# Gated mix of dilated window attention and a spatial-gating MLP: later loads of o and wo, and a maximum in three steps

## The chip, the core and the metric

The kernel runs on one core of a Trainium2 chip. The metric is the device time of one execution in microseconds (us), as the median of several runs. The engines are named as in the profile: PE (TensorE, matrix products; PEld is its weight load), DVE (VectorE), ACT (ScalarE), POOL (GpSimd) and SP (SyncE, which here only issues DMAs). Each takes its instructions in the order of the program; an instruction that waits holds up all those behind it on the same engine. A "q" behind the name (SPq, ACTq) is the engine's sequencer, which issues DMAs and waits.

## The reference

With x of 2048 rows and 1024 columns, all inputs bf16:

```python
g = sigmoid((x * gate_w).sum(-1, keepdims=True))
# A: 32 heads of 32; each position sees 8 keys, at its own place and 2, 4, ... 14 before it
q, k, v = split(x @ wqkv)
attn = softmax(where(in_range, einsum(q, k[window]) * 32 ** -0.5, -1e9))
a = (attn @ v[window]) @ wo
# B: a gated MLP with a 2048x2048 mixing over positions
z1, z2 = split(gelu(x @ w_in))                 # 1792 columns each
b = (z1 * (w_sp @ layernorm(z2) + b_sp[:, None])) @ w_out
out = g * a + (1 - g) * b
```

## The kernel before

**Stages on PE.** The order is: q, k, v for eight groups of four heads (`qkv_tile`, line 739) with part of z2 (`z2_tile`, line 339); the rest of z2; z1 (line 836); the mixing w_sp @ z2 (`g_group`, from about 366 us); the product of the attention's result o with wo (`wo_group`, from about 541 us); the product with w_out (from about 589 us). The last three do a 2x2 block product in seven products instead of eight, with sums and differences of blocks (s1 to s4, t1 to t4, h1 to h4) formed by DVE. All their matmuls are on line 853, in `product`.

**The attention** is not on PE. DVE does it for the eight head groups with multiplications and pairwise sums (lines 362 to 408), spread over the PE stages up to the middle of the mixing. `soft_a` takes the maximum over the 8 keys of a position and subtracts it; `att_L` holds 2 halves x 8 keys x 32 values in each of 128 partitions, in f32, and `att_m` is a small tile of 2 x 4 x 32 values, which `soft_b` uses later for the sums. The results of the groups go to DRAM (`o_d`) by `store_o`, from where transposing DMAs bring them back for `wo_group`: `load_heads(u, r)` on line 492, two for each of eight row blocks u.

**The mixing** has 16 groups n (u = n // 2 is the block of 256 rows, fb = n % 2 the half of the columns). Each group makes seven products of 8 matmuls, in the order a11, s1, s2, a12 (in the bank named `seed`), s3, s4, a22. ACT copies intermediate results out of PSUM (lines 877, 863, 865, 896, 865, 907). DVE adds two pairs (`vec`, line 869) and multiplies with z1 (line 908). The results sit in four ring slots (`g_ring`, which `y_ring` overlays). `y_finish(u)` scales the two groups of block u (lines 701 to 709), and `y_done(u)` stores them to `y_d` (line 652, two DMAs). The copy on line 896 is the first write of a group into its ring slot, so it needs the y store of the group four before it to have landed. The rows of w_sp for the next block come in by two transposing DMAs, `load_rows` on line 597; DVE scales them (`scale_rows`, line 604) and forms s1 to s4 (lines 608 and 609) before the block's first group.

**The order of the work** is fixed when the program is built. A planner, `Beat`, keeps a model clock `now` that moves on by each product's columns (1.52 us for each product of the mixing) and a model time `vector` up to which DVE has work. `beat.at(t, fn)` puts a piece of work at the model time t: it is emitted after the first product at whose end the clock has reached t, in order of t. `behind_mult` is a list that is worked off from its front at two places of a group: an entry (t, price, fn) is emitted if the clock has reached t and the price fits into the group's remaining room (7 us at the end of a group with fb = 1, 1.5 us at the end of the others, the rest of that in the middle of the next group). So the times in `attended` decide the place of each piece in the queues of SP, DVE and PE, and nothing of it is decided at run time.

**`attended`** is emitted at the model time 456.68, which is the start of group 9 and 464.5 us in the trace (so model times here are 7.9 us before the trace's). It stores the last group's o, loads wo, from a copy in DRAM whose rows were put in order earlier (2 MB, `load_wo`, line 566), and plans the loads of the first two blocks of o, the sum for o's scale (`o_total`, `o_matmul`, `o_power`), the scaling of wo in four pieces (`wo_scale`, line 538), the sums for block 0 (`heads_sums(0)`, lines 528 to 532) and two of the four differences of wo (`wo_sum`, line 543).

Of the kernel before, what the change touches and what calls it, by code (L numbers as in the profile page):

```python
# [24 lines left out]
W = 8  # L25
# [36 lines left out]
def kernel(  # L62
# [13 lines left out]
    nc = tc.nc  # L76
# [11 lines left out]
    def reg(off, n):  # L88
        return arena[:, off:off + n]
# [64 lines left out]
    att_m = sm.tile([P, 2, 4, 32], F32, name="att_m")  # L154
# [155 lines left out]
    beat = Beat()  # L310
# [40 lines left out]
    L = att_L  # L351
    L4 = L[:].rearrange("p (a w n) -> p a w n", a=2, w=W, n=32)
# [3 lines left out]
    TT = nc.vector.tensor_tensor  # L356
# [23 lines left out]
        return [(4.4, mul), (2.3, fold(16)), (1.2, fold(8)), (0.7, fold(4)), (0.4, fold(2)), (0.4, last)]  # L380

    def soft_a():
        nc.vector.tensor_reduce(att_m[:, :, 0, :], L[:].rearrange("p (a w n) -> p a n w", a=2, w=W), AX.X, ALU.max)
        TT(L4, L4, att_m[:, :, 0:1, :].to_broadcast([P, 2, W, 32]), ALU.subtract)

    def soft_exp():
# [34 lines left out]
    def store_o(g):  # L421
        dst = o_d[:, g * C:(g + 1) * C].rearrange("(p j) c -> p j c", j=NJ)
        sync.dma_start(dst, obuf)

    def attention_steps(t):
# [29 lines left out]
        for took, fn in pv_steps(NG - 1, 0) + pv_steps(NG - 1, 1):  # L455
            yield t + 5.0, took, fn
        t = beat.vector
        beat.at(t + 1.0, attended)

    beside_fork, beside_copy, behind_mult = [], [], []  # L460
# [11 lines left out]

    def attended():
        store_o(NG - 1)
        load_wo()
        o_norm(NG - 1, reg(A_OFF + 8192, 2048).rearrange("p (j c) -> p j c", j=NJ))
        prep["attended"] = True
        t = max(beat.now, beat.vector)
        plan_heads(0, t + 5.0, 3.0)
        plan_heads(1, t + 11.0, 3.0)  # L480
        beat.at(t + 5.0, o_total)
        behind_mult.append((t + 14.0, 0.0, o_matmul))
        behind_mult.append((t + 15.0, 0.9, o_power))
        for m in range(4):
            behind_mult.append((t + 10.0, 0.75, lambda m=m: wo_scale(m)))
        behind_mult.append((t + 13.5, 2.45, lambda: heads_sums(0)))
        for m in range(2):
            behind_mult.append((t + 13.5, 1.25, lambda m=m: wo_sum(m)))

    def load_heads(u, r):  # L490
        a = 2 * u + r
        sync.dma_start_transpose(heads[u].raw[r], o_d[a * P:(a + 1) * P, :])  # L492

    def plan_heads(u, t, pace):
        for r in range(2):
            beat.at(t + pace * r, lambda r=r: load_heads(u, r))

    def o_norm(g, waste):
        nc.scalar.activation(waste, obuf, ACT.Abs, accum_out=ol[:, g:g + 1])
# [26 lines left out]
    def heads_sums(u):  # L526
        v = heads[u]
        nc.vector.tensor_scalar(v.half, v.flat, osc[:, u:u + 1], None, ALU.mult)
        TT(v.s1, v.a21, v.a22, ALU.add)
        TT(v.s3, v.a11, v.a21, ALU.subtract)  # L530
        TT(v.s2, v.s1, v.a11, ALU.subtract)
        TT(v.s4, v.a12, v.s2, ALU.subtract)
        beat.on_vector(2.45)
        prep["heads"] += 1

    def wo_scale(m):
        sl = slice(2048 * m, 2048 * (m + 1))
        nc.vector.tensor_scalar(wo_h[:, sl], wo_n[:, sl], wsc[:, 1:2], None, ALU.mult)
        beat.on_vector(0.75)

    def wo_sum(m):
        out_, a, b = ((h1, c12, c11), (h2, c22, h1), (h3, c22, c12), (h4, c21, h2))[m]
        TT(out_, a, b, ALU.subtract)
        beat.on_vector(1.25)
# [20 lines left out]
    def load_wo():  # L565
        sync.dma_start(wo_n.rearrange("p (k n) -> p k n", n=D), wop_d.rearrange("(k p) n -> p k n", p=P))
# [197 lines left out]
    for n in range(L1_EARLY):  # L764
        t = beat.now + 8.0 + 13.0 * n
# [19 lines left out]
    t = beat.now  # L785
# [17 lines left out]
    for i in range(16):  # L803
        for c in range(1 if i > 2 else 2, 4):
            z2_tile(i, c)
        n = L1_EARLY + (i - 3) // 2
# [7 lines left out]
    t = beat.now  # L814
# [128 lines left out]
    for n in range(2 * NU):  # L943
        u, fb = n // 2, n % 2
        t = beat.now
# [23 lines left out]
    t = beat.now  # L969
# [174 lines left out]
```

## Time and profile before

| | us |
|---|---|
| median of 3 runs | 679.54 |
| lowest and highest | 678.07, 680.69 |
| the profiled execution's own time | 679.48 |
| its span, first to last instruction | 677.7 |
| PE busy in the span | 670.1 (99%) |
| DVE busy | 537.5 (79%) |
| ACT busy | 381.1 (56%) |
| TensorE clock granted, mean | 1.000 |

The times of rows in the trace are counted from the span's start. The profiled execution's time is 1.8 us longer than its span, and 0.06 us below the median. In a row of the timeline the columns are start, duration, engine, line and operation, what it writes and reads, the number of instructions merged into the row; in brackets how long the engine was idle before it and what ended that. A SPq row is a DMA's issue, not its transfer. "Landing" is the time at which the DMA's semaphore tells that all its data has arrived.

### The profile page before, as it was taken

How to read it: one execution, taken by the hardware profiler on the slowest of the kernel's cores; microseconds unless marked ns; L12 is line 12 of the kernel's file. 1: busy time of each engine (PE TensorE's matmuls, PEld its weight loads, DVE VectorE, ACT ScalarE, POOL GpSimd, SP SyncE). 2: the span in 40 equal slices, each digit the busy share in tenths (PEclk: the TensorE clock that was granted, in tenths of full speed). 3: DMA queues.
4: the chain of work that ended last, by engine and by line, in shares of the span. 5: the costliest groups of instructions: out<-in, count | busy, mean ns of one | idle time of the engine just before them, and what ended most of it. 6: DMA issues, size and time to landing. Idle time of an engine off the chain costs nothing.

```text
span 677.7 us, 9532 instructions
## 1 busy us (share of the span) xinstructions
PE 670.1 (99%) x3587; PEld 392.5 (58%) x3587; DVE 537.5 (79%) x588; ACT 381.1 (56%) x714; POOL 15.5 (2%) x68
## 2 busy tenths in 40 slices
PE   8999999999999999999999999999899999999997
PEld 4568688888885555555555555555455544444443
DVE  1007799999999999999999999997369587954745
ACT  4334646455645985979953666667555574522121
POOL 0000000000000002010100000000000000000000
PEclk9999999999999999999999999999999999999999
DMA  8979869988879754267545555949966699485211
GB/s 233 179 151 281 222 163 289 236 221 219 199 195 241 231 191 175 83 204 251 169 158 176 138 133 148 270 109 248 250 161 164 166 235 251 78 172 144 59 62 63
DMA packets 230734, 123.92 MB, mean 183 GB/s; under 512 B 191008, under 2 KB 217248, under 8 KB 230688
## 3 DMA queue, kind: packets, MB, share of 16 engines
q1 hardware_dynamic: 229104, 121.21, 68.6%
q10 hardware_dynamic: 1584, 2.10, 0.9%
q8 instruction: 28, 0.46, 0.3%
q14 instruction: 18, 0.15, 0.1%
HBM read 63.97 MB, written 37.82 MB: 150 GB/s over the span
## 4 chain that ended last, share of the span: by engine, by line
PE 95%; DMA 2%; SPq 2%; ACT 0%; issue 0%; DVE 0%; ACTq 0%
PE ps L853 36%; PE ps L739 18%; PE ps L339 11%; PE ps L836 11%; PE sd L739 6%; PE seed L853 6%; PE sd L339 4%; PE sd L836 4%; SPq L492 1%; DMA o_d<-arena 1%; DMA arena<-in_B_w_in_dram 1%; DMA y_d<-arena 0%; ACT arena L670 0%; SPq L720 0%; DVE arena L1011 0%
## 5 line engine op out<-in xcount | busy, mean ns | idle before, releaser
L853 PE MATMUL ps<-arena 128*128 128x448 f16 (+1 forms) x1296 | 264.4, 363 | 1.9 <-ACT arena L865 1.9
L853 PEld LDWEIGHTS <-arena 128*128 128x128 f16 x1512 | 147.8, 98 | 156.8 <-issue 2.6
L739 PEld LDWEIGHTS <-arena 128*128 128x128 bf16 x1024 | 141.7, 138 | 24.9
L739 PE MATMUL ps<-arena 128*128 128x384 bf16 x768 | 130.0, 326 | 0.0
L362 DVE TENSOR_TENSOR arena<-arena 128x8192 bf16<-128x8192 bf16 x16 | 70.8, 4422 | 43.9 <-DMA arena<-k_d 43.6
L339 PE MATMUL ps<-arena 128*128 128x448 bf16 (+1 forms) x384 | 77.9, 357 | 0.8 <-DMA arena<-in_B_w_in_dram 0.8
L742 ACT CAST arena<-ps 128x384 bf16<-128x384 f32 x96 | 45.1, 481 | 58.7 <-PE ps L739 58.7
L339 PEld LDWEIGHTS <-arena 128*128 128x128 bf16 x512 | 50.3, 99 | 47.3 <-issue 2.0
L836 PEld LDWEIGHTS <-arena 128*128 128x128 bf16 x512 | 50.0, 98 | 46.6
L366 DVE TENSOR_TENSOR arena<-arena 128x4096 bf16<-128x4096 bf16 (+1 forms) x64 | 74.1, 1158 | 2.0
L836 PE MATMUL ps<-arena 128*128 128x448 bf16 x384 | 75.4, 352 | 0.0
L402 DVE TENSOR_TENSOR arena<-arena,att_A 128x8192 bf16<-128x8192 bf16 x16 | 70.7, 4421 | 0.2
L853 PE MATMUL seed<-arena 128*128 128x448 f16 (+1 forms) x216 | 47.8, 363 | 0.0
L739 PE MATMUL sd<-arena 128*128 128x384 bf16 x256 | 46.8, 326 | 0.0
L408 DVE TENSOR_TENSOR arena<-arena 128x4096 bf16<-128x4096 bf16 x16 | 36.6, 2289 | 0.3
L345 ACT ACTIVATE arena<-ps 128x448 bf16<-128x448 f32 x48 | 26.2, 554 | 17.6 <-PE ps L339 17.3
L572 ACT ACTIVATE arena<-arena 128x2048 bf16<-128x2048 bf16 x16 | 30.8, 1922 | 8.1 <-DMA arena<-in_B_w_sp_dram 8.1
L1075 ACT ACTIVATE arena<-ps,omr 128x512 f32<-128x512 f32 x24 | 16.5, 688 | 32.7 <-PE ps L853 32.7
L839 ACT ACTIVATE arena<-ps 128x448 bf16<-128x448 f32 x48 | 25.1, 557 | 17.1 <-PE ps L836 16.0
L865 ACT ACTIVATE arena<-ps,bt 128x448 f32<-128x448 f32 x32 | 20.3, 634 | 21.9 <-PE ps L853 20.0
L1011 DVE SCALAR_TENSOR_TENSOR arena<-seed,omr,arena 128x512 bf16<-128x512 f32 x8 | 6.0, 750 | 32.7 <-PE seed L853 32.7
L696 ACT ACTIVATE arena<-arena 128x896 bf16<-128x896 bf16 x32 | 30.3, 946 | 1.0 <-DVE arena L908 0.5
(136 smaller groups left out, 602.3 us busy)
## 6 DMA issues: line engine op xcount, KB each, us to landing
arena<-in_B_w_sp_dram SPq DMA_DIRECT2D x16, 512.0 KB, 6.1
arena<-k_d SPq DMA_DIRECT2D x8, 960.0 KB, 7.1
arena<-v_d SPq DMA_DIRECT2D x8, 960.0 KB, 5.3
z_d<-arena SPq DMA_DIRECT2D x16, 448.0 KB, 3.1
arena<-z_d SPq DMA_DIRECT2D x16, 448.0 KB, 4.0
y_d<-arena SPq DMA_DIRECT2D x16, 448.0 KB, 3.6
arena<-in_A_wqkv_dram SPq DMA_DIRECT2D x24, 256.0 KB, 5.6
arena<-in_B_w_in_dram SPq DMA_DIRECT2D x6, 896.0 KB, 5.8
```

What stands on the lines that cost most here:

```text
L339: nc.tensor.matmul(ps[:, 0:N], xT[:, kt, i * P:(i + 1) * P], w2[:, kt, ZC * c:ZC * c + N], start=(kt == 0), stop=(kt == KT - 1))
L345: nc.scalar.activation(z2[:, i, ZC * c:ZC * (c + 1)], ps[:, 0:ZC], ACT.Gelu_apprx_tanh, accum_out=s1[:, 4 * i + c:4 * i + c + 1])
L362: TT(prod.rearrange("p (w j c) -> p w j c", w=W, j=8, c=C), in0, in1, ALU.mult)
L366: return lambda: TT(pv[:, :, 0:n], pv[:, :, 0:n], pv[:, :, n:2 * n], ALU.add)
L402: TT(prod.rearrange("p (w j d h) -> p w j d h", w=W, j=8, d=DH, h=HG), in0, in1, ALU.mult)
L408: return [(4.4, mul), (2.3, lambda: TT(p3[:, 0:4, :], p3[:, 0:4, :], p3[:, 4:8, :], ALU.add)), (1.2, lambda: TT(p3[:, 0:2, :], p3[:, 0:2, ...
L572: nc.scalar.activation(waste, slot, ACT.Abs, accum_out=l1[:, a:a + 1])
L696: nc.scalar.activation(waste, g_ring[n % 4][:, r], ACT.Abs, accum_out=yl[:, k:k + 1])
L739: nc.tensor.matmul(ps[:, 0:3 * C].rearrange("p (t c) -> p t c", t=3), lhsT, wgt[:, :, kt, :], start=(kt == 0), stop=(kt == KT - 1))
L742: nc.scalar.copy(st[:, j % 4, :].rearrange("p (t d h) -> p t d h", t=3, h=HG), ps[:, 0:3 * C].rearrange("p (t h d) -> p t d h", t=3, h=HG))
L836: nc.tensor.matmul(ps[:, 0:512 if whole and kt == 0 else ZC], xT[:, kt, i * P:(i + 1) * P], _sub_ap(w1, kt * ZC, [[1, 512 if whole and kt ...
L853: nc.tensor.matmul(ps[:, 0:c1 - c0], w[:, k, :], v[:, k, c0:c1], start=(first and k == 0), stop=(k == K - 1), skip_group_check=True)
```

## The change

`soft_a` takes the maximum over 8 keys by three element-wise maxima (8 to 4, 4 to 2, 2 to 1), in place of one reduction over a rearranged view. In `attended`, with t the model time there (456.68): the load of wo moves from at once to t + 10.5; the two loads of o's block 0 from t + 5 and t + 8 to t + 7 and t + 10; those of block 1 from t + 11 and t + 14 to t + 16 and t + 19; `o_total` from t + 5 to t + 6. In `behind_mult`, `heads_sums(0)` moves ahead of the four `wo_scale` and is due at t + 18 instead of t + 13.5; the four `wo_scale` are due at t + 24 instead of t + 10, the two `wo_sum` at t + 24 instead of t + 13.5.

```diff
     def soft_a():
-        nc.vector.tensor_reduce(att_m[:, :, 0, :], L[:].rearrange("p (a w n) -> p a n w", a=2, w=W), AX.X, ALU.max)
+        TT(att_m[:], L4[:, :, 0:4, :], L4[:, :, 4:8, :], ALU.max)
+        TT(att_m[:, :, 0:2, :], att_m[:, :, 0:2, :], att_m[:, :, 2:4, :], ALU.max)
+        TT(att_m[:, :, 0:1, :], att_m[:, :, 0:1, :], att_m[:, :, 1:2, :], ALU.max)
         TT(L4, L4, att_m[:, :, 0:1, :].to_broadcast([P, 2, W, 32]), ALU.subtract)
...
     def attended():
         store_o(NG - 1)
-        load_wo()
         o_norm(NG - 1, reg(A_OFF + 8192, 2048).rearrange("p (j c) -> p j c", j=NJ))
         prep["attended"] = True
         t = max(beat.now, beat.vector)
-        plan_heads(0, t + 5.0, 3.0)
-        plan_heads(1, t + 11.0, 3.0)
-        beat.at(t + 5.0, o_total)
+        plan_heads(0, t + 7.0, 3.0)
+        beat.at(t + 10.5, load_wo)
+        plan_heads(1, t + 16.0, 3.0)
+        beat.at(t + 6.0, o_total)
         behind_mult.append((t + 14.0, 0.0, o_matmul))
         behind_mult.append((t + 15.0, 0.9, o_power))
+        behind_mult.append((t + 18.0, 2.45, lambda: heads_sums(0)))
         for m in range(4):
-            behind_mult.append((t + 10.0, 0.75, lambda m=m: wo_scale(m)))
-        behind_mult.append((t + 13.5, 2.45, lambda: heads_sums(0)))
+            behind_mult.append((t + 24.0, 0.75, lambda m=m: wo_scale(m)))
         for m in range(2):
-            behind_mult.append((t + 13.5, 1.25, lambda m=m: wo_sum(m)))
+            behind_mult.append((t + 24.0, 1.25, lambda m=m: wo_sum(m)))
```

## The prediction

> **What bounds the kernel now.** I read the page's busy rows first, then PE's waits, then the chain and the timelines around the only wait that costs anything.
>
> ```profile
> PE 670.1 (99%) x3587; PEld 392.5 (58%) x3587; DVE 537.5 (79%) x588; ACT 381.1 (56%) x714; POOL 15.5 (2%) x68
> ```
>
> PE is busy for 670.1 of 677.7 us. The waits of PE over the whole span are three, and one lies in the part that changes:
>
> ```profile
> PE ps L853 <- ACT arena L865: 1.9, 1, 1.9
> PE pw L114 <- DVE arena L108: 1.2, 1, 1.2
> PE ps L339 <- DMA arena<-in_B_w_in_dram: 0.8, 1, 0.8
> ```
>
> So nothing here can win more than about 2 us. The timeline of PE, with the seed product (the fourth of seven) as a mark for each group, prices it:
>
> ```profile
> 469.08 1.68 PE L853 MATMUL seed<-arena 128*128 128x448 f16 x8
> 479.68 1.68 PE L853 MATMUL seed<-arena 128*128 128x448 f16 x8
> 486.32 6.21 PE L853 MATMUL ps<-arena 128*128 128x448 f16 x32 [1.94 <-ACT arena L865]
> 492.37 1.68 PE L853 MATMUL seed<-arena 128*128 128x448 f16 x8
> 503.02 1.68 PE L853 MATMUL seed<-arena 128*128 128x448 f16 x8
> ```
>
> A group takes 10.60 us (469.08 to 479.68), but 12.69 from group 10's seed to group 11's: 2.1 us lost. The chain of waits says why (SPq L492 are the loads of o):
>
> ```profile
> 465.88 5.16 DMA o_d<-arena
> 471.06 5.80 SPq L492
> 476.91 3.78 SPq L492
> 480.81 2.90 DMA y_d<-arena
> ```
>
> SP waits until the last o is in DRAM (471.04), then spends 5.80 and 3.78 us on issuing the two loads of o's block 0. Behind them stands the y store of block 3, whose data DVE had ready at 474.88 (line 709: 473.60 + 1.28). It lands at 483.7, and ACT's copy into the same ring slot has waited for it:
>
> ```profile
> 483.80 0.53 ACT L896 CAST arena<-seed 128x448 bf16<-128x448 f32 x1 [3.29 <-DMA y_d<-arena]
> 505.72 0.53 ACT L896 CAST arena<-seed 128x448 bf16<-128x448 f32 x1 [1.87 <-DMA y_d<-arena]
> ```
>
> The second row is group 12's: the same kind of wait two groups later, which costs PE nothing so far. What it hangs on is DVE's wait for the rows of w_sp of block 6:
>
> ```profile
> 494.56 1.23 DVE L604 TENSOR_TENSOR arena<-arena,rs_b 128x2048 f16<-128x2048 bf16 x1 [4.21 <-DMA arena<-in_B_w_sp_dram]
> 497.25 1.22 DVE L604 TENSOR_TENSOR arena<-arena,rs_b 128x2048 f16<-128x2048 bf16 x1 [1.46 <-DMA arena<-in_B_w_sp_dram]
> ```
>
> From 497.25 to 530 DVE has no gap, so all it does there, the y store of block 4 included (issued 502.99, landed 505.62), is pinned to the landing of these rows. SP's timeline shows what stood before them:
>
> ```profile
> 466.51 2.54 SPq L566 DMA_DIRECT2D arena<-wop_d  x1
> ...
> 481.89 2.25 SPq L492 DMA_TRANSPOSE arena<-o_d  x1
> 484.19 0.57 SPq L600 DMA_DIRECT2D rs_b<-rs_d  x1
> 484.85 0.38 SPq L646 DMA_DIRECT2D arena<-z_d  x1
> 485.33 8.64 SPq L597 DMA_TRANSPOSE arena<-in_B_w_sp_dram  x2
> ```
>
> **The change, part by part.**
>
> **The maximum.** The reduction (line 383, 400.06) is followed by the next instruction 1.08 us later. The three maxima have the shapes of lines 390 to 392, which take 0.42, 0.29 and 0.23 us and, with their gaps, 1.04 (421.50 to 422.54). If a maximum costs what an addition costs, DVE gains 0.04 us eight times, 0.3 in all. If it ran at the reduction's rate, 1.05 us for 512 elements, 448 elements in three would take 0.92 plus overheads, some 1.1: 0.2 lost in all. Either lies beside PE, which has no wait before 484; DVE ends the attention at 462.83 and soon idles 3.16 us before line 908 (467.06), which covers it. I take nothing.
>
> **Order on DVE and PE.** I followed the planner's arithmetic. `o_total` (t + 6 = 462.68) still comes out after the product that ends at 462.75. `o_matmul` and `o_power` are held by `w_total` and `w_power` ahead of them in the list, until 484.01 and 488.57. At 488.57 the room of 7 us takes `o_power` (0.9), `heads_sums(0)` (2.45) and four `wo_scale` (3.0), as before: only the last two change places, and `wo_sum` stays one group later. The work is the same at the same place: 0. Its inputs keep their cover: in the trace it begins at 506.60, and wo should land before 492 (below).
>
> **Order on SP.** Before: o stored, wo, z1 of group 10, o 0.0, o 0.1, y of block 3 (two DMAs), o 1.0, scale 6, z1 of group 11, rows 6 (two), o 1.1, z1 of group 12. After, by due times against product ends: o 0.0 (463.68) is emitted at 464.27, y 3 (465.18) at 465.79, o 0.1 and wo at 467.31, scale 6 and z1 at 468.83, rows 6 at 470.35, o 1.0 (472.68) at 473.38, o 1.1 at 476.42. So: o stored, z1 10, o 0.0, y 3, o 0.1, wo, scale 6, z1 11, rows 6, o 1.0, o 1.1, z1 12. The y store passes one load of o, not both; but wo is also gone from before it, and the long issue times of L492 are seen only with wo in flight: the other loads of o take 1.24 to 2.9 us, 1.31 in the median.
>
> **The stall.** After: o 0.0 is issued at 471.06 and done by 473.3 (2.25, the row at 481.89). The y store waits for DVE, 474.88, and lands 2.6 to 4.7 later (the spread of such stores), at 477.5 to 479.6. Group 10's copy wants its slot at 480.5 (483.80 - 3.29). The wait of 3.29 goes and PE's 2.1 us with it: -2.1. Behind the waiting y store on SP stand o 0.1, wo and the rows; this wait is part of the next sum.
>
> **What is late next.** o 0.1 follows at 475.9 (landing at 480.4, by the 4.45 of the row at 481.89), wo is issued at 478.3 and its packets follow o's. Before (landings are those of single DMAs in the trace), they began when the queue was clear, near 470.4, and landed at 479.72: 9.3 later. So wo lands at about 489.5; z1 10 landed 1.24 behind it before, so z1 11 lands at about 490.5, against 491.57 now. The rows came 2.9 and 5.6 after z1 11 (494.47 and about 497.2), so they come about 1 us earlier than now: x = -1, as one block of o left the queue ahead of them. Bounds of x: if wo needs only the 4 us that it took for its later three quarters (1.6 MB at the 391 to 407 GB/s of the windows 474 to 478) and 2 for the first quarter (264 GB/s, 472 to 474), -3; if it needs its whole 13.2 from its issue, wo lands at 491.5 and the rows at +1.1; if the rows were then issued only behind it and took their longest 9.1 us, +6. I take -1, from the sum nearest in kind (the same load, FIFO, the same followers).
>
> **What PE then meets.** Let p be PE's shift at group 12. Its a22 product starts at 507.56 + p (504.53 and 16 matmuls of 0.189) and needs line 865, which ends 1.16 after line 896 starts. Line 896 waits for the y store at 505.72 + x. So p is no less than x - 0.63. The s1 product (500.0 + p) needs the sum of line 608, ready at 499.2 + x: p no less than x - 0.8, weaker. With x = -1: p = -1.63. Of the 2.1 us won, 0.5 come back as a wait in group 12. From there on DVE moves with x and PE with p; group 14's copy has over 1 us to spare (first y landing before 525, wanted 525.9). PE runs on to the end without waits, so p is the result.
>
> **Sum.** 679.48 - 2.1 + 0.5 = 677.85. The profiled execution is 0.06 below the median, so I say 677.8.
>
> Trainium skill, *DMA: Bandwidth & Descriptors*, "Where 436 GB/s comes from": a load from HBM is bound by some 358 GB/s for the core. By that, an estimate, 2.1 MB take 5.9 us, x is near -3 and the sum -2.1 (677.4). The trace, with 9.3 us for this load, disagrees, and I go by it.
>
> **Rivals.**
>
> *A, slower: wo now stands in front of the rows.* Its 2 MB move from 19 us ahead of rows 6 to 3.5 us ahead, and the rows end DVE's wait of 4.21 us. For it: DVE already waits there, and L492 behind wo took 5.80 us to issue. Against it: the rows are behind z1 11 and two loads of o now, too. It decides at x above +0.63, where PE loses more at group 12 than it won at group 10. At x = +1.1 the time is 679.48 + 0.5 = 680.0; at x = +6, 684.9. Over 0.5% (3.4 us) it needs x = +4.
> The Trainium skill, same page, "Queues, rings and completion order", says that descriptors of one queue are consumed in ring order, which is this rival's rule; the trace agrees (the y packets of the stalled store run only when o's are through).
>
> *B: the rows are early enough.* With x at -1.5 or less the whole 2.1 us stay: 677.4. For it: wo's faster phase. Against: the 9.3 us.
>
> *C: the change misses the stall.* One load of o stays ahead of the y store. If its issue took 5.80 again without wo, the store would go out at 476.9 and land by 479.8 to 481.6, still nearly in time. It takes over 7.5 us to keep the stall: 679.5.
>
> **How the numbers follow.** Half a per cent, 3.4 us, is about what a measurement of this kernel can tell from no change. Forecast (gain of 0.3 to 2.0) 0.50, B 0.22, C 0.08, A 0.20, of which half over 3.4 us, as its steps are the least known. The forecast's own range is 677.3 to 679.2. With a median's scatter of about 1 us (678.07 to 680.69 before), B reaches down to 676.3 and the smaller half of A up to 681.5: the range 676.3 to 681.5. Faster by over 0.5% (below 676.1) has no mechanism, only scatter: 0.03. Slower: 0.10. Within: 0.87.
>
> **What would show it.** Line 896 of group 10 without a wait, the y store issued at about 475, the seeds of groups 10 and 11 10.6 us apart: the first step right. wo issued near 478 and landing near 489.5, line 604 for rows 6 starting at 493.5 and 496.2: the second. A gap of PE of about 0.5 us before group 12's a22, ended by line 865, and 10.6 per group after it: the third. Wrong it would be if the rows land after 498, if PE waits anywhere past 520, or if the sums of lines 528 to 543 wait for wo.

## The result and the profile after

The changed kernel takes 675.76 us in the median (675.42 to 678.09, 7 runs); the kernel before took 680.28 (678.07 to 681.71, 7 runs, the three given above among them). The ratio is 0.9945, 95% interval 0.9926 to 0.9964. The profiled execution takes 675.6 us, its span is 673.7, against 679.48 and 677.7 before: 4.0 us less, where 1.6 were forecast. Lines behind 386 have moved by two: 853 is now 855, 896 is 898, and so on.

The timeline of PE, in the stretch shown before, has no gap between the seeds of groups 10 and 11 (477.36 to 487.95, 10.59 us), and a small one in group 12:

```profile
466.77 1.68 PE L855 MATMUL seed<-arena 128*128 128x448 f16 x8
477.36 1.68 PE L855 MATMUL seed<-arena 128*128 128x448 f16 x8
487.95 1.68 PE L855 MATMUL seed<-arena 128*128 128x448 f16 x8
495.97 3.20 PE L855 MATMUL ps<-arena 128*128 128x448 f16 x16 [0.23 <-DVE arena L610]
499.01 1.68 PE L855 MATMUL seed<-arena 128*128 128x448 f16 x8
```

Group 9's seed comes at 466.77, though, against 469.08 before. That is 2.31 us earlier in a stretch that the new order of SP has not reached yet. From there to group 12's seed it is 32.24 us, against 33.94 before: 1.70 us less. So the 4.0 us are two things. SP's timeline after the change shows the second:

```profile
463.41 0.58 SPq L425 DMA_DIRECT2D o_d<-arena  x1
465.86 0.85 SPq L648 DMA_DIRECT2D arena<-z_d  x1
468.72 1.27 SPq L494 DMA_TRANSPOSE arena<-o_d  x1
472.62 1.60 SPq L654 DMA_DIRECT2D y_d<-arena  x2
474.28 1.47 SPq L494 DMA_TRANSPOSE arena<-o_d  x1
475.80 0.59 SPq L568 DMA_DIRECT2D arena<-wop_d  x1
476.43 0.58 SPq L602 DMA_DIRECT2D rs_b<-rs_d  x1
477.11 0.49 SPq L648 DMA_DIRECT2D arena<-z_d  x1
477.69 13.33 SPq L599 DMA_TRANSPOSE arena<-in_B_w_sp_dram  x2
```

The first load of o takes 1.27 us to issue instead of 5.80, the y store (line 654) follows when DVE has its data, and the long issue is now that of the rows of w_sp, behind wo: 13.33 us for two, against 8.64. On ACT the copy of group 10 (first row) no longer waits for a store; that of group 12 waits longer than before, 2.58 us for 1.87:

```profile
479.07 0.53 ACT L898 CAST arena<-seed 128x448 bf16<-128x448 f32 x1 [0.88 <-PE seed L855]
...
502.42 0.53 ACT L898 CAST arena<-seed 128x448 bf16<-128x448 f32 x1 [2.58 <-DMA y_d<-arena]
```

The other 2.31 us lie at the start. The next rows are PE's first products, before and then after the change; the text behind an "x" is the number of matmuls, and the rows with `sd` are single matmuls of 448 columns:

```profile
5.81 1.28 PE L339 MATMUL ps<-arena 128*128 128x448 bf16 x3 [0.78 <-DMA arena<-in_B_w_in_dram]
6.89 0.58 PE L339 MATMUL sd<-arena 128*128 128x448 bf16 x1
...
8.60 0.58 PE L339 MATMUL sd<-arena 128*128 128x448 bf16 x1
...
10.03 0.35 PE L339 MATMUL sd<-arena 128*128 128x448 bf16 x1
```

```profile
5.26 0.86 PE L339 MATMUL ps<-arena 128*128 128x448 bf16 x3
5.95 0.35 PE L339 MATMUL sd<-arena 128*128 128x448 bf16 x1
...
7.80 0.35 PE L339 MATMUL sd<-arena 128*128 128x448 bf16 x1
```

A matmul of the same shape takes 0.58 us until about 9.7 us in the profile of before, and 0.35 from 5.6 on in that of after. The third `sd` product starts at 10.03 and at 7.80, so 2.23 of the 2.31 us are there. The trace's record of the granted TensorE clock begins to show the full clock at 9.74 and at 5.55. Whether this belongs to the change was the first thing to find out.

### The profile page after: what moved, and what is told of

Read it like the earlier page. It is cut to its first block, busy times and chain, and to the rows that moved or that the text cites. A ratio compares the mean times of both kernels' runs of the same rounds, so it can differ in the third digit from the quotient of the medians.

```text
span 673.7 us, 9548 instructions
## 1 busy us (share of the span) xinstructions
PE 668.4 (99%) x3587; PEld 391.8 (58%) x3587; DVE 536.7 (80%) x604; ACT 380.9 (57%) x714; POOL 15.4 (2%) x68
## 4 chain that ended last, share of the span: by engine, by line
PE 98%; DMA 1%; DVE 0%; SPq 0%; issue 0%
PE ps L855 38%; PE ps L741 19%; PE ps L339 11%; PE ps L838 11%; PE seed L855 6%; PE sd L741 6%; PE sd L339 4%; PE sd L838 4%; DMA arena<-in_B_w_sp_dram 1%; DMA arena<-in_B_w_in_dram 1%; DVE arena L606 0%; SPq L722 0%; DVE arena L1013 0%; DVE arena L610 0%; PE pt L320 0%
```

## The experiments

Two theories. Q: SP's order gives some 1.7 us, and the start is drawn anew in each run, whatever the kernel. S: the start belongs to the change. Both unchanged kernels and the two halves of the change ran on one chip. A quoted text stands as it was written before its run; each ratio is to 31 or 32 runs of the kernel before, measured beside it.

### The kernel before once more

> The kernel before, unchanged, once more. Theory Q (queue order): of the 4.0 us between the two profiled spans, 1.7 us come from SP's order around groups 10 to 12, and 2.3 us from the moment at which the full TensorE clock is granted at the start (9.74 us before, 5.55 us after), which changes from run to run and not with the kernel. Then here the grant comes at either time, with times of about 677.5 (early) or 679.8 (late), group 10 to group 11 takes 12.7 us in either, and the ratio to the kernel before is 1.000 within 0.002. Rival S (the start belongs to the change): every run of the kernel before has the late grant, near 9.7 us, and about 680.

Measured: 677.35 us in the median of 12 runs (676.84 to 679.52), ratio to the runs of before beside it 0.9985 (0.9968 to 1.0001). Its profile has the full clock at 6.02 us and a span of 675.7, 2.0 us less than the first profile of the same kernel. PE's timeline shows the same loss at group 10 as before (2.18 us from seed to seed, beyond 10.59):

```profile
477.64 1.68 PE L853 MATMUL seed<-arena 128*128 128x448 f16 x8
479.15 3.19 PE L853 MATMUL ps<-arena 128*128 128x448 f16 x16
484.36 6.21 PE L853 MATMUL ps<-arena 128*128 128x448 f16 x32 [2.02 <-ACT arena L865]
490.41 1.68 PE L853 MATMUL seed<-arena 128*128 128x448 f16 x8
```

Eight runs lie from 676.84 to 677.78, four from 678.82 to 679.52. The early clock is there without the change: S falls. The control also says how far a ratio of this kernel can be off: 0.15% from itself.

### The changed kernel once more

> The changed kernel, unchanged, once more. Theory Q: early or late grant as in the kernel before, so times of 675.6 or 677.9, seeds of groups 10 and 11 10.6 us apart, 0.4 us lost in group 12; ratio over many runs nearer to 0.9975 (the queue alone) than to 0.9945. Rival S: the early grant always, 675.6, ratio 0.994 again.

Measured: 675.94 us (675.15 to 678.15, 12 runs), ratio 0.9959 (0.9943 to 0.9975). Again eight runs in a lower level (675.15 to 676.00) and four above (677.12 to 678.15): the same shares as the control. Median to median these two kernels are 1.41 us apart, lowest to lowest 1.69. In this profile group 12 loses nothing (seeds at 488.64 and 499.28), though its copy waits 2.33 us for the y store. The forecast that the ratio would move to 0.9975 is met against the control (675.94 / 677.35 = 0.9979), not against the shared runs of before (0.9959).

### The two halves of the change

```diff
 max_only: in soft_a of the kernel before
-        nc.vector.tensor_reduce(att_m[:, :, 0, :], ..., AX.X, ALU.max)
+        TT(att_m[:], L4[:, :, 0:4, :], L4[:, :, 4:8, :], ALU.max)
+        ...
 queue_only: attended as changed, soft_a as before
```

> Only the maximum in three operations; the queue as before. Theory Q: no change, 1.000 within 0.002; group 10 to 11 still 12.7 us; eight maxima save DVE some 0.3 us that nothing waits for. Rival S in its one form that has a place (16 more instructions on DVE shift the program): the early grant in nearly all runs, 2.3 us faster, ratio 0.9966.

> Only the later loads and their work; the maximum by one reduction. Theory Q: the same as the whole change at equal grant, so group 10 to 11 at 10.6 us, group 12 losing about 0.4, ratio as that of the whole change in this same call within 0.002. Rival S with the maximum as the cause: late grants, 677.9, ratio 0.9975, and the whole change 2.3 us faster.

Measured: the maximum alone 677.58 us, 0.9997 (0.9979 to 1.0014); the queue alone 675.69 us, 0.9961 (0.9942 to 0.9979), where the whole change had 0.9959 against the same runs of before. So the queue is all of it, as far as intervals of about 0.002 to either side can tell. In DVE's timeline of the changed kernel the three maxima take what was worked out: the next instruction, line 386, begins 1.04 us after the first, against 1.08 with the reduction.

```profile
397.52 0.42 DVE L383 TENSOR_TENSOR att_m<-att_L 128x256 f32<-128x256 f32 x1
397.98 0.29 DVE L384 TENSOR_TENSOR att_m<-att_m 128x128 f32<-128x128 f32 x1
398.30 0.22 DVE L385 TENSOR_TENSOR att_m<-att_m 128x64 f32<-128x64 f32 x1
398.56 0.69 DVE L386 TENSOR_TENSOR att_L<-att_L,att_m 128x512 f32<-128x512 f32 x1
```

One point missed: group 10 to 11 took 11.74 us in the profile of the maximum alone, not 12.7. The loss before the change is not one number: 2.1, 2.2 and 1.15 us in three profiles with the old order. In these wo lands 13.2, 13.4 and 12.5 us after its issue, and the y store of block 3 lands 4.0 to 4.1 us after wo.

### Which of the moved loads it is

```diff
 o_only: from the kernel before
-        plan_heads(0, t + 5.0, 3.0)
-        plan_heads(1, t + 11.0, 3.0)
+        plan_heads(0, t + 7.0, 3.0)
+        plan_heads(1, t + 16.0, 3.0)
 wo_only: from the kernel before
-        load_wo()
+        beat.at(t + 10.5, load_wo)
```

> From the kernel before, only the loads of o moved (t + 7, t + 10, t + 16, t + 19); wo is loaded at once, as before. The y store of block 3 then stands behind wo and one load of o, not two. If SP's issue of the o loads is what holds it (issue theory), it goes out 3.8 us earlier than before, group 10's copy waits for nothing and group 10 to 11 takes 10.6 us. If the transfer queue is what holds it (queue theory: everything behind wo waits for its 2 MB), its data moves only 1.4 us earlier, the copy still waits some 2 us, and 0.5 to 1 us of the 2.1 stay lost. Rows 6 land about 2 us earlier than before, so group 12 loses nothing in either.

> From the kernel before, only the load of wo moved to t + 10.5; all loads of o at their old times. Both loads of block 0 then stand ahead of the y store, but without wo in the queue. Expected: 1.3 us of issue each, the y store goes out when DVE has its data, group 10 to 11 at 10.6 us. Block 1's first load stands before the rows of block 6 again: these land some 1.2 us later than with the whole change, and group 12 loses 0.8 to 1.6 us where the whole change loses 0 to 0.4. Rival (the position of the o loads is what counts): the copy of group 10 waits over 2 us.

Measured, the loads of o alone: 677.89 us (10 runs), 0.9992 (0.9971 to 1.0012), no gain clear of the noise. SP's timeline and PE's wait:

```profile
464.57 2.68 SPq L566 DMA_DIRECT2D arena<-wop_d  x1
467.37 0.93 SPq L646 DMA_DIRECT2D arena<-z_d  x1
469.27 5.68 SPq L492 DMA_TRANSPOSE arena<-o_d  x1
475.06 1.89 SPq L652 DMA_DIRECT2D y_d<-arena  x2
```

```profile
PE ps L853 <- ACT arena L865: 1.1, 1, 1.1
```

The y store goes out at 475.06, 5.8 us after the load of o in front of it began to issue, as against 9.7 in the profile of before (471.06 to 480.81); and still the copy of group 10 waits 2.47 us (until 481.22; 0.88 is usual) and group 10 to 11 takes 11.87. The issue theory said 10.6; the queue theory said a loss of 0.5 to 1, and 1.27 was measured, which is no less than the smallest loss with the old order. The chain of waits decides for the queue. The first row is the y store in it for the loads of o alone, the second for the maximum alone, which has the old order:

```profile
475.06 6.07 DMA y_d<-arena
478.12 2.88 DMA y_d<-arena
```

Issued 3.06 us earlier, it landed at 481.1 against 481.0. wo had landed at 478.1 and at 476.9. So the store's data had to wait for wo's, whenever it was issued. Group 12 loses nothing here, as both said.

Measured, wo alone: 676.32 us (10 runs), 0.9970 (0.9951 to 0.9989). In SP's timeline both loads of block 0 stand before the y store, and issue in 2.61 us:

```profile
469.83 2.61 SPq L492 DMA_TRANSPOSE arena<-o_d  x2
473.38 0.91 SPq L652 DMA_DIRECT2D y_d<-arena  x2
474.33 1.76 SPq L566 DMA_DIRECT2D arena<-wop_d  x1
476.15 4.40 SPq L492 DMA_TRANSPOSE arena<-o_d  x1
```

Group 10 to 11 takes 10.59 us. So wo's place ahead of the y store is the cause of the loss, and the place of the o loads is not. A smaller loss comes back in group 12, in its a22 product, and by the way that was forecast: its copy waits 2.98 us for the y store and line 865 ends PE's wait. It is 0.40 us (seeds at 499.35 and 510.34) where 0.8 to 1.6 were expected. PE's timeline:

```profile
504.29 6.21 PE L853 MATMUL ps<-arena 128*128 128x448 f16 x32 [0.23 <-ACT arena L865]
```

### wo behind the rows

```diff
-        beat.at(t + 10.5, load_wo)
+        beat.at(t + 13.0, load_wo)
```

> The whole change with wo at t + 13.0 instead of t + 10.5, which puts it behind the rows of block 6 on SP. If wo's 2 MB are what holds the rows back, these land some 5 us or more earlier, DVE no longer waits for them, the y store of block 4 goes out early enough for group 12's copy to wait for nothing, and group 12 loses nothing: 0 to 0.4 us faster than the whole change at the same start. wo is still in time for its scaling. If the rows are bound by their own transfer or by PE's use of their buffer, they land as before.

Measured: 676.45 us (675.17 to 677.69, 12 runs), 0.9965 (0.9949 to 0.9981). SP issues the rows at 477.40 in 7.63 us, and wo after them (first fence, SP's timeline; the second is DVE's); line 606 has no wait for the rows and scales them at 486.15, against 491.25 and 493.96 in the profile of the changed kernel; the copy of group 12 waits only its usual 0.88 us; group 11 to 12 takes 10.64 us, which is what it takes with nothing lost.

```profile
477.40 7.63 SPq L599 DMA_TRANSPOSE arena<-in_B_w_sp_dram  x2
485.08 0.57 SPq L568 DMA_DIRECT2D arena<-wop_d  x1
485.70 8.24 SPq L494 DMA_TRANSPOSE arena<-o_d  x2
```

```profile
486.15 2.36 DVE L606 TENSOR_TENSOR arena<-arena,rs_b 128x2048 f16<-128x2048 bf16 x2
```

So it was wo that held the rows. The long issue has moved on to the loads of o's block 1, which nobody waits for. The time itself does not tell this version from the whole change: half of its runs fell into the upper level.

### Taking the start out

The levels are as far apart as what is to be measured, so the last runs change the start. Two more warm-up matmuls go between the first transposes and the first product (`..._fill`); `after_cold` has two at the very start instead of six. `best_fill` is wo behind the rows with the fill, and `best_fill_2` is the same kernel again. The quoted texts below are in the order of the table.

```diff
         for kt in range(ahead):
             turn(kt)
+        if ahead:
+            pw = seeded.tile([P, 512], F32, name="pw", tag="sd")
+            for _ in range(2):
+                nc.tensor.matmul(pw[:], warm[:, 0:P], warm, start=True, stop=True)
 ...
 after_cold: from the changed kernel
-    warm_up(6)
+    warm_up(2)
```

> The version with wo behind the rows, and two more warm-up matmuls (512 columns) on PE between the first three pairs of transposes and the first product, where PE idles for 0.1 to 1.1 us at the start. Theory: the late grant of the full clock comes from a gap in PE's work in the first 6 us; without the gap the late times (2.3 us above the others) get rare, and the median is at the early level or up to 0.7 us above it, as the added matmuls take 0.43 us each at the slow clock. If the grant's time is not set by such a gap, early and late times stay as frequent as without.

> The kernel before with the two added warm-up matmuls alone. Clock theory: its late times (near 679.5) go and the early ones stay: median 676.9 to 677.4, spread about 1.2 us, ratio to the kernel before 0.998. If the rarity of late times with the fill so far was chance or belonged to wo behind the rows, the two levels stay.

> The whole change with the two added matmuls. Clock theory: one level, median 675.2 to 675.7. Its distance to the kernel before with the same fill is then the queue's part alone: 1.4 to 2.1 us, 0.21 to 0.31%.

> wo behind the rows, with the fill, once more, beside the whole change with the fill: 0 to 0.4 us faster than that (the group 12 wait), 675.0 to 675.6.

> The whole change with two warm-up matmuls at the start in place of six, so that PE idles from about 2 to 4 us. Clock theory: the full clock is granted after 7 us in nearly all runs, and the level is the late one, 677.4 to 678.5, with few runs at 675.6. If the late level has another cause (the input transfers), the levels stay mixed as in the whole change: two runs in three near 675.7.

| kernel | median us (runs) | lowest, highest | ratio to before, interval |
|---|---|---|---|
| best_fill | 675.53 (9) | 674.78, 676.01 | 0.9956, 0.9939 to 0.9974 |
| before_fill | 677.82 (12) | 677.30, 680.82 | 0.9988, 0.9970 to 1.0007 |
| after_fill | 675.89 (12) | 675.57, 676.86 | 0.9962, 0.9948 to 0.9977 |
| best_fill_2 | 675.46 (8) | 675.06, 676.05 | 0.9947, 0.9930 to 0.9964 |
| after_cold | 677.33 (12) | 676.22, 679.74 | 0.9978, 0.9959 to 0.9997 |

With the new order and the fill there is one level: 29 runs within 674.78 to 676.86. Without it, 13 of 39 runs of the changed kernel, the queue alone and wo behind the rows lie at 676.9 or above. PE's timeline at the start of best_fill, where its gap is down from 0.78 to 0.46 us and the full clock is there by the first product:

```profile
4.58 0.65 PE L337 MATMUL pw<-arena 128*128 128x512 bf16 x2
5.07 0.28 PE L320 MATMUL pt<-ident,arena 128*128 128x128 bf16 x2
5.80 0.73 PE L343 MATMUL ps<-arena 128*128 128x448 bf16 x3 [0.46 <-DMA arena<-in_B_w_in_dram]
```

With less warm-up the median rises by 1.4 us over the changed kernel's (675.94, on another chip). In its PE timeline there is a wait of 1.21 us early, the first products run at 0.58 us, and the full clock comes at 7.71:

```profile
3.42 0.29 PE L320 MATMUL pt<-ident,arena 128*128 128x128 bf16 x1 [1.21 <-DMA arena<-in_A_x_dram]
...
5.39 1.28 PE L339 MATMUL ps<-arena 128*128 128x448 bf16 x3 [0.27 <-DMA arena<-in_B_w_in_dram]
6.46 0.58 PE L339 MATMUL sd<-arena 128*128 128x448 bf16 x1
```

That profile is of a run at 676.22; of the 12 runs three lie in the expected 677.4 to 678.5, two above and seven below, so the warm-up moves the times but does not fix them.

The clock theory is borne out in part only. The fill takes the upper level away. But in the profile of best_fill_2 PE has no wait after its first matmul, and the full clock still comes at 7.19; in that of after_cold it comes at 7.71. Neither run is in an upper level (676.05 and 676.22 us). In the profile of the changed kernel once more it comes at 3.93, and PE then waits 0.57 and 1.07 us for its inputs. So a gap alone does not set the moment, and the first profile, with 9.74, is the only one kept of a run in an upper level.

The kernel before with the fill missed its expectation: seven runs lie from 677.30 to 677.85, but five from 678.87 to 680.82. So the old order has long times that this fill does not take away, and with the new order it leaves none.

The granted clock tells these apart. Four of the five (679.15 to 680.82) have a mean granted clock of 0.996 or 0.997; every other run of the table has 0.999 or 1.000. This is not the late start, which the mean does not contain: the first profile has 1.000, with the full clock at 9.74. An estimate from these figures: 0.3% of 678 us are 2.0 us. The same holds wherever wo was loaded at once. Of the 140 runs of the experiments with that order (the kernel before, with and without the fill, the maximum alone, the loads of o alone), 36 have 0.996 or 0.997, at 678.98 to 682.02 us, in the mean 2.6 us above the other 104. Of all 90 runs with wo moved, none has less than 0.999. So the old order has a second loss, in about a quarter of its runs, and it is gone where wo is moved. Where in the run the clock is lower is not shown, as every profile kept has 0.999 or more. Nor is it shown that PE's idle 1 to 2 us at group 10 is the cause.

The mean of before_fill, 678.47, is 2.43 us above after_fill's 676.04, its median 1.93, its lowest 1.73. Without the four runs its mean is 677.72, 1.68 above, which is the 1.7 us of the order. Its profile, of a run at 677.44, loses 2.28 us at group 10.

The version with wo behind the rows and the fill is 0.43 us below the whole change with the fill in the median, measured beside it, where the profile of the latter loses 0.54 us from group 11 to 13. It has the lowest medians of all versions here, at 0.9956 and 0.9947 of the kernel before.

## Why the prediction was right, and where it was off

**The stall and its end: right.** The wait of 3.29 us on the copy went, and with it the 2.1 us of group 10. The y store was forecast for 474.88 and goes out at 472.62, which with the 2.31 us of the start is 474.93. One number in it was wrong without consequence: the copy was said to want its slot at 480.5 (483.80 - 3.29), but 0.88 us of that idle time is its usual wait for PE, so it wanted it at 481.4.

**What is late next: right.** With the same 2.31 us added, wo is issued at 478.11 (478.3 forecast), z1 of group 11 lands at 490.93 (490.5; the profile gives no landing of wo itself), and DVE starts on the two halves of the rows at 493.56 and 496.27 (493.5 and 496.2). x was taken as -1 from the landing times of the same load before; it is -1.0, and -1.6 to -1.7 in the second profile. The estimate from the Trainium skill's rate (*DMA: Bandwidth & Descriptors*, "Where 436 GB/s comes from"), which made x -3, is not borne out.

**What PE meets in group 12: right in size, not in the place.** p was -1.63 by the forecast and is -1.70. The wait came at the s1 product, behind the sum of line 610, and not before a22 behind the copy; the two bounds lie 0.17 apart, and the copy's proved the looser. The copy can wait 2.33 us (0.88 of it usual) at no cost to PE, and 2.60 at a cost of 0.02 (the queue alone), in line with the 1.87 + 0.63 used. In other draws of the same order group 12 loses nothing, or 0.5 us. None of the three signs of being wrong came: the rows landed before 498, PE waits nowhere past 520, and the sums of lines 530 to 545 do not wait for wo.

**Rival A** was real as a mechanism, but x stayed below its +0.63; the rows' issue did grow, to 13.33 us. **Rival C** fell: the o load ahead of the store issues in 1.27 us without wo. (Two slips on the way change nothing: a gain of 0.3 to 2.0 gives 677.5 to 679.2, not 677.3, and the store of rival C would land from 479.5, not 479.8.)

**The maximum: right**, 0.

**The sum: its base was off.** The step that failed is "679.48 - 2.1 + 0.5": it took the profiled execution of before as typical of every run. That execution had the late clock, in rows that the forecast did not read, since PE counts as busy there. At an early clock the kernel before has 677.5 and the changed one 675.6 to 675.9. The span of 4.0 us less is 1.7 from the order and 2.3 from the start. The measured 675.76 lies 2.0 below the forecast for this reason, and 0.5 below the lower end of the range; and the ratio of 0.9945 holds some luck: four of the seven runs of before lie at 680.28 or more, where all later runs with that order have the lower granted clock, while five of the seven of the changed kernel lie in its lower level. The second measurement's ratio is 0.9959, and against the unchanged kernel as a control it is 0.9979.

**The chance of 0.03 for over 0.5% faster** rested on the claim that nothing but scatter could add to 2.1 us. The scatter was known to be about 1 us from three runs; it is up to 2.3 us for the start alone, and in about a quarter of its runs the old order takes some 2 us more, at a lower granted clock, for which the prediction had no term.

## What to carry to other kernels

A large load that is wanted late is not free when issued early: everything behind it on the queue waits for its bytes, and the price is paid at the first urgent transfer, here a store of a buffer that was to be written again. To judge a move in a queue, list what stands behind the moved transfer and when each of these is wanted, and then do it again for the place to which it moves. Compare two profiles stage by stage before adding up their spans: a difference that begins long before the place that was to change needs a run of the unchanged kernel beside it, before it is put down to the change. And look at the granted clock of all runs, not only at that of the one with a profile.

## What the runs showed of the hardware

The full clock of TensorE is granted between 3.93 and 9.74 us after the start, for the same first instructions of PE. In the profile with 9.74, group 9's seed comes 1.6 to 2.3 us later than in the others without the fill and with the usual warm-up (469.08 against 466.77 to 467.52). The Trainium skill, *TensorE: Matmul & The Clock Gate*, Part 1, says that the time of this grant changes from run to run, because the activity window runs freely. The traces agree that it changes, but not in the size: the page has it vary by 500 ns to either side, and here it varies by nearly 6 us. What was not expected is that the spread is as large as the gain of a queue change, that the times come in two levels, and that two matmuls in a gap of some 0.1 to 1.3 us remove the upper one in 29 runs of 29 with the new order.

A mean granted clock of 0.996 or 0.997 came in 36 of 140 runs with wo loaded at once and in none of 90 with wo moved; its cause is open.

A transposing DMA behind a large load holds its queue's sequencer for longer: 1.26 us of issue without wo in flight, 5.68 and 5.80 soon behind it, 13.33 for the two of the rows, and 8.24 for two loads of o when these came next.
